# One gather for two sequences and an earlier transposition of K at the start of a block-sparse attention with a routed MLP

## The chip, the core and the metric

The kernel runs on one core of one Trainium2 chip, in float32. The metric is the device time of one execution in microseconds (us). A profiled execution gives the trace from which the details come.

## What is computed

Two stages follow each other. The first is BigBird attention over 4 sequences (batch), 8 heads, 768 positions and 64 features per head. Positions come in 24 blocks of 32. A query block sees its own block and both neighbours, the first and the last block, and three random blocks; the first and the last query block see everything.

```python
mask = np.abs(blk_i - blk_j) <= window
mask = mask | (blk_i == 0) | (blk_j == 0) | (blk_i == n_blocks - 1) | (blk_j == n_blocks - 1)
for qb in range(n_blocks):
    for kb in sampled_blocks[qb]:
        mask[qb*block:(qb+1)*block, kb*block:(kb+1)*block] = True
...
attn = np.exp(scores)
attn = attn / (np.sum(attn, axis=-1, keepdims=True) + 1e-09)
return np.matmul(attn, v)
```

The second stage takes the 3072 rows of 512 features, picks for each the expert (of 8) whose embedding has the largest cosine with it, and computes `gate * (relu(x @ w1[e]) @ w2[e])` with 1024 hidden features.

## The kernel before

The attention works in 24 steps, one for each chunk of 128 queries of one sequence. Sequences go in pairs: a step number maps to a chunk and to one of the two sequences of the pair. The order of the first steps is written out in `TURNS`: step 0 is chunk 0 of sequence 0, step 1 chunk 1 of sequence 0, step 2 chunk 0 of sequence 1, step 3 chunk 1 of sequence 1; after that the two sequences alternate. Steps are pipelined: in step s the scores of chunk s are made (`score_near`, lines 549 and 552, and `score_far`, line 574), those of chunk s-1 are multiplied with V (`weigh_near`, `weigh_far`, `weigh_ends`, all through line 629), normalized (`normalize`, lines 680 to 698), and those of chunk s-2 are turned (`turn_x`, line 706) and multiplied with the experts' embeddings (`chunk_logits`, line 717). For chunk 0, whose first block sees all keys, there are `score_ends` (lines 596 to 607) and `weigh_ends` too.

The program's order on each engine is the order in which the code is written; nothing reorders it. [...]

What feeds the steps:

- `load_k` and `turn_k`: K of a pair of heads comes into `kraw` (6 buffers) and is turned by 6 transposes on TensorE (line 500) into a PSUM tile of the ring "big", which has two buffers and also holds every score tile. DVE (even pairs) or ACT (odd pairs) copies it to `kt` (line 502); after the fourth pair of a sequence ACT copies the first and last block behind it (line 505). Pairs 0 to 3 are sequence 0, pairs 4 to 7 sequence 1. Before the change, pairs 4 to 7 are turned at the end of step 1.
- `gather_k`: K of the random blocks, copied within SBUF by DVE and POOL (lines 531, 535).
- `gather_v`: V of the random blocks straight from device memory into the ring `vg` (two buffers, one per chunk of a pair), one transfer for each random slot and each block (line 477), with the block number read into SP's registers first (line 377). The argument `i` limits it to one of the two sequences. A chunk has 4 blocks and 3 slots, so 12 transfers; chunk 0 has 6, as two of its blocks are not gathered.
- `load_v`: V in full, into `vt`, one tile for each chunk; `stack`, `stack_ends` and `near_v` copy from it what the neighbours and ends need.
- `load_q` and `turn_q`: Q into `qraw` (two buffers), turned on TensorE (line 513) and copied by DVE into `qt` (line 518).

All of these transfers except the first three of Q are issued from SP's queue by `fetch_all` (lines 475, 477, 479), which can put a load between each second gather. The queue ahead of the first steps is written out: gathers of chunk 0 for sequence 0; V tiles 2 to 5 of sequence 0; K of pairs 6 and 7; gathers of chunk 1 for sequence 0, with Q of sequence 1 between; V tiles 0 and 1 of sequence 1; gathers of chunk 0 for sequence 1; V tiles 2 to 5 of sequence 1; gathers of chunk 1 for sequence 1; a row of zeros to `x_dram` (line 1314). Behind them come step 2's loads: Q of the next chunks and K of pairs 8 and 9.

`build_experts` is a generator that is advanced between the steps: it normalizes the 8 embeddings and turns them (line 232) into `en`, in two halves that share one PSUM bank, each followed by a copy on DVE (line 234).

After the attention, expert tiles of 128 rows run (lines 1152 and 1165), with weights streamed from device memory.

Of the kernel before, what the change touches and what calls it, by code (L numbers as in the profile page):

```python
# [12 lines left out]
F32 = mybir.dt.float32  # L13
I32 = mybir.dt.int32
BF16 = mybir.dt.bfloat16
ACT = mybir.ActivationFunctionType
# [4 lines left out]
P = 128  # L21
# [4 lines left out]
NC = S // P  # L26
NPAIR = H // 2
N = B * S
NT = B * NC
DM, E, F = H * D, 8, 1024  # L30
ND, NF = DM // P, F // P
# [38 lines left out]
def bank(k, name):  # L70
    if k.attending:
        return ring(k, "yp", 0, 1, k.eps, [P, DM])
    return two_banks(k, name)[:, 0]
# [141 lines left out]
def build_experts(k):  # L215

    nc, pool = k.nc, k.setup
    emb, tau = k.emb_rows, k.tau_rows
    sq = pool.tile([E, DM], F32, name="emb_sq")
    nrm = pool.tile([E, 1], F32, name="emb_nrm")  # L220
    nc.scalar.activation(sq, emb, ACT.Square, accum_out=nrm)
    nc.gpsimd.tensor_tensor(out=nrm, in0=nrm, in1=k.half[0:E, 0:1], op=ALU.pow)
    yield
    nc.vector.tensor_scalar(out=nrm, in0=nrm, scalar1=1e-6, scalar2=tau[:, 0:1], op0=ALU.add, op1=ALU.mult)
    nc.vector.reciprocal(out=nrm, in_=nrm)
    nc.vector.tensor_scalar(out=emb, in0=emb, scalar1=nrm[:, 0:1], scalar2=None, op0=ALU.mult)
    yield
    k.en = k.const.tile([P, ND, E], F32, name="en")
    for some in (range(2), range(2, ND)):
        tp = bank(k, "tp")  # L230
        for c in some:
            nc.tensor.transpose(tp[:, c * E:(c + 1) * E], emb[:, c * P:(c + 1) * P], k.ident[0:E, 0:E])
        cols = slice(some.start * E, some.stop * E)
        nc.vector.tensor_copy(out=k.en.rearrange("p c e -> p (c e)")[:, cols], in_=tp[:, cols])
        yield


def load_pair(k, g, parts=(0, 1, 2)):
# [171 lines left out]
def load_q(k, s, i=None):  # L410

    a, c = pair_chunk(s)
    if ("q", s) not in k.raw:
        k.raw["q", s] = k.ld.tile([P, DUO, H, D], F32, name="qraw", tag="qraw", bufs=2)
    t, src = in_pair(k.raw["q", s], i), of_seq(k.q, a, i)
    return [(t[rows], src[lo:lo + rows.stop - rows.start]) for rows, lo in pieces(c)]
# [9 lines left out]
def load_v(k, a, m, i=None):  # L426

    v, src = in_pair(k.vt[m], i), of_seq(k.v, a, i)
    return [(v[rows, :, 0:D], src[lo:lo + rows.stop - rows.start]) for rows, lo in pieces(m)]
# [32 lines left out]
def gather_v(k, s, i=None):  # L462

    a, c = pair_chunk(s)
    t, src = k.vg_ring[s % 2], of_seq(k.v, a, i)
    for r in range(NRAND):
        for g, shift in zip(blocks_of(c), shifts(k, mybir.EngineType.SP, r, c)):
            yield in_pair(t[r * BLK:(r + 1) * BLK, g], i)[:, :, 0:D], src[bass.ds(shift, BLK)]


def fetch_all(k, gathers, loads):

    for i, (to, src) in enumerate(gathers):
        if i % 2 == 0 and loads:
            k.nc.sync.dma_start(out=loads[0][0], in_=loads[0][1])
            loads = loads[1:]
        k.nc.sync.dma_start(out=to, in_=src)  # L477
    for to, src in loads:
        k.nc.sync.dma_start(out=to, in_=src)
# [12 lines left out]
def turn_k(k, g):  # L492

    nc = k.nc
    b, j = divmod(g, NPAIR)
    kt = k.kt[b % 2]
    raw = k.raw.pop(("k", g))
    ps = k.big.tile([P, 2, 512], F32, name="kps", tag="big")
    for c in range(NC):
        nc.tensor.transpose(ps[:, c // 3, c % 3 * P:(c % 3 + 1) * P], raw[:, c].rearrange("p h d -> p (h d)"), k.ident)  # L500
    copy = nc.scalar.copy if g % 2 else nc.vector.tensor_copy
    copy(out=kt[:, j, 0:S].rearrange("p (w t) -> p w t", w=2), in_=ps[:, :, 0:3 * P])  # L502
    if j == NPAIR - 1:
        for i, block in enumerate((NB - 1, 0)):
            nc.scalar.copy(out=kt[:, :, S + i * BLK:S + (i + 1) * BLK], in_=kt[:, :, block * BLK:(block + 1) * BLK])  # L505
# [132 lines left out]
def weigh_near(k, n, turn):  # L638

    _, c, i = place(n)  # L640
    if turn == 0:
        k.av[n] = two_banks(k, "av"), set()
    e, st = k.pac[n], k.st_ring[n // DUO % 2]
    for hh in range(2 * turn, 2 * turn + 2):
        for h in (hh, hh + NPAIR):
            for half in (1,) if c == 0 else (0, 1):
                to = side(c, h, half)
                weigh(k, n, slice(D * to, D * (to + 1)), h, e[:, h // 2, half, D * (h % 2):D * (h % 2 + 1)],
                      st[:, half, i, h], turn == 1)
    if turn == 1:  # L650
        k.pac.pop(n)


def weigh_far(k, n, part):
# [14 lines left out]
def normalize(k, n):  # L669

    nc = k.nc
    b, c, i = place(n)
    s = n // DUO
    if i == 0:
        k.x[s] = k.xp.tile([P, DUO, ND, XE], F32, name="x", tag="x")
        k.nsq[s] = k.xp.tile([P, DUO], F32, name="nsq", tag="nsq")
        k.lg[s] = k.xp.tile([P, DUO, E], F32, name="lg", tag="lg")
    av = k.av.pop(n)[0].rearrange("p g (h w) -> p (g h) w", w=P)
    den = k.dens[:, n, :]
    nc.vector.tensor_scalar(out=den, in0=av[:, :, D], scalar1=1e-9, scalar2=None, op0=ALU.add)  # L680
    inv = k.xt_pool.tile([P, H], F32, name="inv", tag="inv")
    nc.vector.reciprocal(out=inv, in_=den)
    x = k.x[s][:, i, :, 0:P].rearrange("p j (h d) -> p j h d", h=2)
    half = NPAIR // 2
    if c:
        todo = [(slice(0, P), slice(0, P), slice(0, NPAIR))]
    else:
        todo = [(slice(0, P), slice(0, P), slice(0, half)), (slice(0, D), slice(D, P), slice(half, NPAIR)),
                (slice(D, P), slice(0, D), slice(half, NPAIR))]
    for to, at, pairs in todo:  # L690
        heads = slice(2 * pairs.start, 2 * pairs.stop)
        count = pairs.stop - pairs.start
        nc.vector.tensor_tensor(  # L693
            out=x[to, pairs], in0=av[at, heads, 0:D].rearrange("p (j h) d -> p j h d", h=2),
            in1=inv[at, heads].rearrange("p (j h) -> p j h", h=2).unsqueeze(3).broadcast_to(
                [at.stop - at.start, count, 2, D]), op=ALU.mult)
    sq = k.xt_pool.tile([P, ND, P], F32, name="sq", tag="sq", bufs=1)
    nc.scalar.activation(sq, k.x[s][:, i, :, 0:P], ACT.Square, accum_out=k.nsq[s][:, i:i + 1])


def turn_x(k, n):

    s, i = divmod(n, DUO)
    ps = ring(k, "xg_ps", 0, 1, k.eps, [P, ND, P])
    for j in range(ND):
        k.nc.tensor.transpose(ps[:, j], k.x[s][:, i, j, 0:P], k.ident)  # L706
    k.xt[n] = t = k.xt_pool.tile([P, ND, P], F32, name="xt", tag="xt")
    k.nc.vector.tensor_copy(out=t, in_=ps)  # L708
# [535 lines left out]
def attention_fast(n, ctx):  # L1244
# [3 lines left out]
    nc = n.nc  # L1248
# [36 lines left out]
    for vg in n.vg_ring:  # L1285
        nc.gpsimd.memset(vg[:, :, :, :, D:D + 1], 1.0)
    build_choice(n)
    fetch_all(n, gather_v(n, 0, 0), [])
    for m in range(2, NC):
        fetch_all(n, (), load_v(n, 0, m, 0))  # L1290
    turn_q(n, 0)
    for g in range(NPAIR):
        turn_k(n, g)
        if g + 6 < 2 * NPAIR:
            fetch_all(n, (), load_k(n, g + 6))
    fetch_all(n, gather_v(n, 1, 0), load_q(n, 0, 1) + load_q(n, 1, 1))
    for m in range(2):
        fetch_all(n, (), load_v(n, 0, m, 1))
    fetch_all(n, gather_v(n, 0, 1), [])
    for m in range(2, NC):  # L1300
        fetch_all(n, (), load_v(n, 0, m, 1))
    fetch_all(n, gather_v(n, 1, 1), [])
    build_bias(n)
    gather_k(n, 0)
    n.half = n.const.tile([P, NC], F32, name="half")
# [1 line left out]
    experts = build_experts(n)  # L1307
# [5 lines left out]
    nc.gpsimd.memset(zero, 0.0)  # L1313
    nc.sync.dma_start(n.x_dram[N:N + 1, :], zero)

    turning = {10: (8, 9), 11: (10, 11, 12), 12: (13, 14, 15)}
    keys_at = {2: (8, 9), 3: (10,), 4: (11,), 5: (12,), 6: (13,), 10: (14, 15)}
    values_at = {7: (0,), 8: (1,), 9: (2,), 11: (3,), 13: (4,), 15: (5,)}
    routed = {TURNS.index(DUO * b + 1) + 2: b for b in range(NS - 1)}
# [1 line left out]
    for s in range(NCH + 1):  # L1321
        now, after, last, past = (TURNS[i] if 0 <= i < NCH else None for i in (s, s + 1, s - 1, s - 2))
# [8 lines left out]
        def keys_gathered():  # L1331
            if after is not None:
                gather_k(n, after)

        ends = last is not None and place(last)[1] == 0
        late_keys = s == 1 or s in turning
        if now is not None:
            score_near(n, now)
            score_far(n, now)
# [26 lines left out]
            score_ends(n, last, 2)  # L1366
        if past is not None:
            turn_x(n, past)
        for g in turning.get(s, ()):
            turn_k(n, g)  # L1370
        if s in turning:
            keys_gathered()
        for part in range(2):
            if last is not None:
                weigh_far(n, last, part)
            if after is not None and part == 0 and not ends:
                turn_q(n, after)
        if ends:
            weigh_ends(n, last, (0, 2))
# [36 lines left out]
            build_consts(n)  # L1416
            next(experts)
        if s == 1:
            for g in range(NPAIR, 2 * NPAIR):
                turn_k(n, g)  # L1420
            keys_gathered()
            next(experts)
            next(experts)
            setup.close()
            n.dp = pool("dp_e", 1)
# [228 lines left out]
```

## Time and profile before

| | |
|---|---|
| median of 3 runs | 645.87 us (643.56 to 647.22) |
| profiled execution | 645.84 us |
| its span | 644.0 us |
| TensorE busy | 607.3 us, 94% of the span |
| DVE, ACT, POOL busy | 37%, 22%, 38% |
| mean granted TensorE clock | 0.976 |
| attention steps | up to about 290 us |
| DMA moved | 170.57 MB in 187,599 packets, 148,008 of them under 512 B |

The profile page gives busy times by engine, the chain of work that ended last, and groups of instructions by source line. A line of the timeline reads: start, length, engine, source line, operation, output<-inputs, shape, count, and in brackets the idle time before it with what ended it. "PE" is TensorE's matmuls (transposes among them), "PEld" its weight loads, "SPq" the issuing of DMAs by SP's queue: its length is the time that the queue was held, not that of the transfer.

### The profile page before, as it was taken

How to read it: one execution, taken by the hardware profiler on the slowest of the kernel's cores; microseconds unless marked ns; L12 is line 12 of the kernel's file. 1: busy time of each engine (PE TensorE's matmuls, PEld its weight loads, DVE VectorE, ACT ScalarE, POOL GpSimd, SP SyncE). 2: the span in 40 equal slices, each digit the busy share in tenths (PEclk: the TensorE clock that was granted, in tenths of full speed). 3: DMA queues.
4: the chain of work that ended last, by engine and by line, in shares of the span. 5: the costliest groups of instructions: out<-in, count | busy, mean ns of one | idle time of the engine just before them, and what ended most of it. 6: DMA issues, size and time to landing. Idle time of an engine off the chain costs nothing.

```text
span 644.0 us, 18357 instructions
## 1 busy us (share of the span) xinstructions
PE 607.3 (94%) x7496; PEld 471.4 (73%) x7496; DVE 235.6 (37%) x740; ACT 141.6 (22%) x286; POOL 244.5 (38%) x472
## 2 busy tenths in 40 slices
PE   6879889899999999999999999999999999999995
PEld 3668878798899888887777777663677746667773
DVE  3545544656666675236622111221121121211110
ACT  1534444554554444210000000000000000000000
POOL 1618246534766532031033444333334433333332
PEclk7899979999999799999999999999999999999998
DMA  9877999999999994079999999999899998999611
GB/s 170 170 150 152 177 170 170 183 185 175 182 191 184 178 162 145 36 278 401 396 406 394 406 399 365 341 320 375 308 395 410 396 375 308 413 390 408 247 48 34
DMA packets 187599, 170.57 MB, mean 265 GB/s; under 512 B 148008, under 2 KB 148136, under 8 KB 184690
## 3 DMA queue, kind: packets, MB, share of 16 engines
q1 hardware_dynamic: 180194, 155.35, 84.8%
q0 software_dynamic: 5216, 13.43, 5.7%
q8 instruction: 61, 1.00, 0.7%
q10 hardware_dynamic: 2096, 0.52, 0.5%
q14 instruction: 32, 0.26, 0.2%
HBM read 156.65 MB, written 12.90 MB: 263 GB/s over the span
## 4 chain that ended last, share of the span: by engine, by line
PE 75%; DMA 7%; SPq 6%; DVE 5%; issue 2%; POOL 2%; ACT 1%; POOLq 0%; DVEq 0%; ACTq 0%
PE hp L1152 25%; PE yp L1165 23%; PE av L629 6%; SPq L477 5%; PE dps L574 4%; PE yp L717 3%; DMA vg<-in_v_dram 3%; PE hp L1197 2%; PE yp L1217 2%; PE ac L549 2%; PE xg_ps L513 2%; PE ac L552 2%; DMA w<-in_moe_w_dram 2%; DMA qraw<-in_q_dram 1%; DMA kraw<-in_k_dram 1%
## 5 line engine op out<-in xcount | busy, mean ns | idle before, releaser
L1152 PEld LDWEIGHTS hp<-xgt,w 128*128 128x128 f32 x1472 | 167.8, 192 | 11.5 <-issue 10.2
L1152 PE MATMUL hp<-xgt,w 128*128 128x128 f32 x1472 | 169.2, 275 | 1.0 <-DMA w<-in_moe_w_dram 1.0
L1165 PE MATMUL yp<-w,h 128*128 128x512 f32 x368 | 161.9, 592 | 0.0
L1165 PEld LDWEIGHTS yp<-w,h 128*128 128x128 f32 x368 | 68.1, 190 | 76.5 <-issue 72.0
L1076 POOL DMA_INDIRECT xg<-x_dram,quarter x88 | 89.4, 1016 | 32.3 <-issue 27.4
L1178 POOL DMA_INDIRECT out_dram<-y,slot_l x20 | 20.5, 1026 | 155.8 <-DVE y L1177 155.8
L1155 ACT ACTIVATE h<-hp 128x512 f32<-128x512 f32 x23 | 13.7, 597 | 284.1 <-PE hp L1152 226.6
L1159 DVE TENSOR_SCALAR h<-hp 128x512 f32<-128x512 f32 x23 | 15.9, 692 | 145.1 <-PE hp L1152 145.1
L489 POOL COPY vg<-vt 32x1040 f32<-32x1040 f32 (+1 forms) x45 | 43.1, 958 | 57.2 <-PE av L629 45.0
L531 POOL COPY kg<-kt 128x128 f32 x176 | 43.2, 291 | 45.5 <-ACT kt L502 38.0
L549 PE MATMUL ac<-qt,kt 128*64 128x128 f32 x352 | 47.0, 290 | 3.3 <-DVE qt L518 3.3
L574 PEld LDWEIGHTS dps<-qt,kg 128*64 128x64 f32 x1408 | 48.2, 142 | 0.8 <-POOL vg L489 0.8
L574 PE MATMUL dps<-qt,kg 128*64 128x64 f32 x1408 | 46.9, 226 | 0.5 <-DVE kg L531 0.5
L552 PE MATMUL ac<-qt,kt 128*64 128x256 f32 (+1 forms) x192 | 46.4, 389 | 0.8 <-ACT kt L505 0.8
L518 DVE COPY qt<-xg_ps 64x512 f32<-64x512 f32 x48 | 33.0, 688 | 36.3 <-PE xg_ps L513 36.0
L1177 DVE TENSOR_SCALAR y<-yp,gate 128x512 f32<-128x512 f32 x20 | 15.0, 751 | 85.0 <-PE yp L1165 72.9
L549 PEld LDWEIGHTS ac<-qt,kt 128*64 128x64 f32 x352 | 41.5, 147 | 4.2 <-ACT st L441 1.8
L579 ACT ACTIVATE pd<-dps,bias 128x256 f32<-128x256 f32 x88 | 34.7, 475 | 15.8 <-PE dps L574 15.8
L629 PE MATMUL av<-vg,pd 128*32 128x65 f32 x1408 | 32.4, 225 | 3.5 <-DMA vg<-in_v_dram 2.8
L629 PE MATMUL av<-st,pac 128*64 128x65 f32 x704 | 31.0, 229 | 2.3 <-DVE x L693 1.3
L629 PEld LDWEIGHTS av<-vg,pd 128*32 128x32 f32 x1408 | 23.8, 110 | 12.1 <-issue 8.8
L708 DVE COPY xt<-xg_ps 128x512 f32<-128x512 f32 x24 | 16.6, 690 | 31.8 <-PE xg_ps L706 31.7
(229 smaller groups left out, 633.7 us busy)
## 6 DMA issues: line engine op xcount, KB each, us to landing
w<-in_moe_w_dram SPq DMA_DIRECT2D x52, 2048.0 KB
vg<-in_v_dram SPq DMA_DIRECT2D x114, 128.0 KB
kraw<-in_k_dram SPq DMA_DIRECT2D x32, 192.0 KB
x_dram<-x SPq DMA_DIRECT2D x10, 516.0 KB
qraw<-in_q_dram SPq DMA_DIRECT2D x9, 512.0 KB
w<-in_moe_w_dram SPq DMA_DIRECT2D x8, 512.0 KB
vt<-in_v_dram SPq DMA_DIRECT2D x10, 256.0 KB
vt<-in_v_dram SPq DMA_DIRECT2D x5, 512.0 KB
```

The lines of the kernel that those rows point to most:

```text
L477: k.nc.sync.dma_start(out=to, in_=src)
L489: k.nc.gpsimd.tensor_copy(out=k.vg_ring[s % 2][NRAND * BLK:P, g, which(i)], in_=k.vt[m][rows, which(i)])
L518: k.nc.vector.tensor_copy(out=t[rows, :, h], in_=ps[rows])
L531: copy(out=t[:, :, g, s * BLK:(s + 1) * BLK], in_=kt[:, :, bass.ds(shift, BLK)])
L549: nc.tensor.matmul(out[0:D, j, half], lhsT=kt[:, j, at:at + D], rhs=qt[:, j, :, D * half:D * (half + 1)], start=True, stop=True)
L552: nc.tensor.matmul(out[D:P, j, half:2].rearrange("p f h t -> p h f t"), lhsT=kt[:, j, S:S + D], rhs=qt[:, j, :, D * half:P].rearrange("p h ...
L574: nc.tensor.matmul(out[D * r:D * (r + 1), NG * j + g], lhsT=kg[:, j, g, D * r:D * (r + 1)], rhs=qt[:, j, :, cols], start=True, stop=True)
L579: nc.scalar.activation(e[:, :, g].rearrange("p j h t -> p j (h t)"), out.rearrange("p (j g) h t -> p j g (h t)", g=NG)[:, :, g], ACT.Exp, ...
L629: k.nc.tensor.matmul(av[lanes, h // NPAIR, h % NPAIR * P:h % NPAIR * P + D + 1], lhsT=lhsT, rhs=rhs, start=first[0], stop=last, skip_group ...
L1076: k.nc.gpsimd.indirect_dma_start(out=x[:, g], out_offset=None, in_=quarters, in_offset=bass.IndirectOffsetOnAxis(ap=k.quarter[:, g, t:t + ...
L1152: nc.tensor.matmul(hp[:, f, :], lhsT=w1[:, d, (f0 + f) * P:(f0 + f + 1) * P], rhs=xt[:, d, :], start=(d == 0), stop=(d == ND - 1))
L1165: nc.tensor.matmul(yp, lhsT=h[:, f, :], rhs=w2[:, f, :], start=(f == 0), stop=(f == NF - 1))
```

## The change

Three edits, and one that makes room. (a) `gather_v` is called without `i` for the first two chunks, so that one transfer brings a block for both sequences (32 rows x 16 heads x 64 features instead of 32 x 8 x 64); V of sequence 1 follows all gathers. (b) K of sequence 1 is turned in the middle of steps 0 (pairs 4, 5) and 1 (pairs 6, 7), where before all four pairs were turned at the end of step 1; in step 0 `turn_q` moves ahead of it, and in step 1 the gather of K for step 2 follows it. (c) The embeddings are turned into one PSUM bank at once and copied once. The squares that `normalize` makes only for their sum are written over the used probabilities (`pac`) instead of a tile of their own.

```diff
-    for some in (range(2), range(2, ND)):
-        tp = bank(k, "tp")
-        for c in some:
-            nc.tensor.transpose(tp[:, c * E:(c + 1) * E], emb[:, c * P:(c + 1) * P], k.ident[0:E, 0:E])
-        cols = slice(some.start * E, some.stop * E)
-        nc.vector.tensor_copy(out=k.en.rearrange("p c e -> p (c e)")[:, cols], in_=tp[:, cols])
-        yield
+    tp = bank(k, "tp")
+    for c in range(ND):
+        nc.tensor.transpose(tp[:, c * E:(c + 1) * E], emb[:, c * P:(c + 1) * P], k.ident[0:E, 0:E])
+    nc.vector.tensor_copy(out=k.en.rearrange("p c e -> p (c e)"), in_=tp[:, 0:ND * E])
+    yield
...
-    if turn == 1:
-        k.pac.pop(n)
...
-    sq = k.xt_pool.tile([P, ND, P], F32, name="sq", tag="sq", bufs=1)
-    nc.scalar.activation(sq, k.x[s][:, i, :, 0:P], ACT.Square, accum_out=k.nsq[s][:, i:i + 1])
+    used = k.pac.pop(n)[:, 0:NPAIR:2].rearrange("p j f w -> p j (f w)")
+    nc.scalar.activation(used.rearrange("p j (e w) -> p j e w", w=P),
+                         k.x[s][:, i, :, 0:P].rearrange("p (j e) w -> p j e w", e=2), ACT.Square,
+                         accum_out=k.nsq[s][:, i:i + 1])
...
-    fetch_all(n, gather_v(n, 0, 0), [])
+    fetch_all(n, gather_v(n, 0), [])
...
-    fetch_all(n, gather_v(n, 1, 0), load_q(n, 0, 1) + load_q(n, 1, 1))
-    for m in range(2):
+    fetch_all(n, gather_v(n, 1), load_q(n, 0, 1) + load_q(n, 1, 1))
+    for m in range(NC):
         fetch_all(n, (), load_v(n, 0, m, 1))
-    fetch_all(n, gather_v(n, 0, 1), [])
-    for m in range(2, NC):
-        fetch_all(n, (), load_v(n, 0, m, 1))
-    fetch_all(n, gather_v(n, 1, 1), [])
...
-    turning = {10: (8, 9), 11: (10, 11, 12), 12: (13, 14, 15)}
+    turning = {0: (4, 5), 1: (6, 7), 10: (8, 9), 11: (10, 11, 12), 12: (13, 14, 15)}
...
-        late_keys = s == 1 or s in turning
+        late_keys = s in turning and s > 0
...
+        if s == 0:
+            turn_q(n, after)
         for g in turning.get(s, ()):
             turn_k(n, g)
-        if s in turning:
+        if late_keys:
             keys_gathered()
         for part in range(2):
             if last is not None:
                 weigh_far(n, last, part)
-            if after is not None and part == 0 and not ends:
+            if after is not None and s and part == 0 and not ends:
                 turn_q(n, after)
...
         if s == 1:
-            for g in range(NPAIR, 2 * NPAIR):
-                turn_k(n, g)
-            keys_gathered()
-            next(experts)
             next(experts)
```

## Prediction

> **What bounds the kernel now.** I read the chain of waits first. Most of it is TensorE work, with a DMA share, and 6% of the span in which the chain runs through SP's own queue, nearly all in line 477, the V gathers.
>
> ```profile
> PE 75%; DMA 7%; SPq 6%; DVE 5%; issue 2%; POOL 2%; ACT 1%; POOLq 0%; DVEq 0%; ACTq 0%
> ```
>
> Next came windows over the places where TensorE (PE) falls idle. Columns: stretch, its length, busy us (instructions) of PE, weight loads, DVE, ACT, POOL, then PE's granted clock, DMA share, GB/s.
>
> ```profile
> 40.00:47.00 7.00, 3.91 (x39) 3.36 (x37) 4.84 (x14) 2.70 (x6) 1.63 (x7) 1.00 0.67 144
> 61.00:67.00 6.00, 4.01 (x109) 3.57 (x108) 0.00 (x0) 1.72 (x3) 2.17 (x3) 1.00 0.84 183
> 83.00:87.00 4.00, 1.82 (x36) 1.14 (x35) 0.78 (x2) 2.77 (x5) 3.71 (x11) 1.00 1.25 185
> 87.00:94.00 7.00, 7.00 (x81) 6.61 (x81) 3.81 (x15) 0.99 (x4) 0.62 (x3) 0.52 1.34 169
> ```
>
> PE has holes at 40-47, 61-67 and 83-87, and right after the third its clock is about half for 7 us while it is fully busy. The timeline of PE names the holes (start, length, line, idle before it and its releaser):
>
> ```profile
> 37.70 0.63 PE L513 MATMUL xg_ps<-ident,qraw 128*128 128x128 f32 x4 [1.54 <-DMA qraw<-in_q_dram]
> ...
> 40.04 1.53 PE L500 MATMUL kps<-ident,kraw 128*128 128x128 f32 x12
> 42.94 1.53 PE L500 MATMUL kps<-ident,kraw 128*128 128x128 f32 x12 [1.37 <-DVE kt L502]
> 44.40 0.29 PE L232 MATMUL yp<-ident,emb 8*128 8x8 f32 x2
> 46.40 0.29 PE L232 MATMUL yp<-ident,emb 8*128 8x8 f32 x2 [1.72 <-DVE en L234]
> ```
>
> ```profile
> 83.76 0.27 PE L629 MATMUL av<-vg,pd 128*32 128x65 f32 x2 [0.54 <-DMA vg<-in_v_dram]
> 84.66 0.27 PE L629 MATMUL av<-vg,pd 128*32 128x65 f32 x2 [0.62 <-DMA vg<-in_v_dram]
> 85.40 0.27 PE L629 MATMUL av<-vg,pd 128*32 128x65 f32 x2 [0.47 <-DMA vg<-in_v_dram]
> 86.22 0.61 PE L629 MATMUL av<-vg,pd 128*32 128x65 f32 x26 [0.54 <-POOL kg L531]
> ```
>
> At 40-47 four K transposes and the two embedding halves stand in a row at the end of step 1, and step 2 starts its scores only at 46.62. The fourth row at 86 is named for POOL, but its weight load also waits on the last gather (landed 86.08 by the trace's semaphore updates), so I count all four, 2.2 us, as gathers that came late. Why they were late shows in SP's timeline:
>
> ```profile
> 48.60 3.07 SPq L479 DMA_DIRECT2D vt<-in_v_dram  x4
> 51.87 9.04 SPq L477 DMA_DIRECT2D vg<-in_v_dram  x12
> 61.01 0.29 SPq L1314 DMA_DIRECT2D x_dram<-zero  x1
> 61.39 0.41 SPq L479 DMA_DIRECT2D qraw<-in_q_dram  x1
> ```
>
> Four 256 KB loads leave in 3.07 us, but twelve 64 KB gathers take 9.04, 0.75 us each, while the 16 DMA engines are only 0.63 busy at 53-61. SP's issuing is the limit there. Behind it stands the q load of step 2, which leaves at 61.39 and lands at 66.93; PE waits 1.91 us for it at 67.06.
>
> **What the skill says.** "DMA: Bandwidth & Descriptors", section Rules for kernel authors: many small transfers should be coalesced, since "under 64 KB you're paying mostly overhead". This trace agrees: 0.75 us of queue for 64 KB against 0.77 for 256 KB. "Perfetto Trace Analysis", DMA Instruction — HWDGE: the recorded time of an issue covers lock, descriptor generation and semaphore push, not the data movement. Agrees: the q load issues in 0.41 us and lands 5.5 us after. "TensorE: Matmul & The Clock Gate", Part 1, says PE's clock halves after an idle window of about 3.4 us and is judged in free-running windows of 3413 ns. The trace agrees in form: the clock records hold half speed from 87.25 to 94.08, twice 3.41 us, right after the window 83.84-87.25 in which PE was 52% busy. But windows of 51% and 55% (42.88-46.29, 36.05-39.46) were not followed by it, so the threshold is not plain.
>
> **The change, part by part.** The sum is made against the profiled execution: 645.84 us, span 644.0, so 1.8 around it; the median of the three runs is 645.87, the same within 0.1.
>
> *Gathers for both sequences.* 36 gathers of 64 KB become 18 of 128 KB, and two of the eight register loads on SP (median 0.39) go. The shortest issue is 0.316 us in both sizes (the gathers of 19-61, and the 128 KB ones of 82-130); with 0.18 us of register work each pair of issues is 0.50 us apart when nothing blocks. Upper bound: 18 x 0.50 + 0.8 = 9.8 us of SP queue saved. Lower bound: none, if a transfer costs by its bytes. By bytes, 128 KB take 0.58 us (256 B packets take 18-19 ns on each of 16 engines), so the set stays near its issue rate and I take 7.5. The q load of step 2 then leaves near 54 and lands near 59. PE wants it at 65.15 minus what it gains before, so 3 us of saving suffice. The six gathers of chunk 0 now carry 384 KB more ahead of K of pairs 6 and 7; they leave at their old times (19.1 to 22.7, set by register loads), the data end about 0.4 us later. Packet count and bytes stay.
>
> *V of sequence 1* moves behind all gathers: its last load leaves near 47 instead of 51.7, its first near 42.5 as now. Wanted at 58: nothing.
>
> *K of pairs 4, 5 in step 0.* PE 2 x 0.77 after the q transposes at 22.56-23.22. Cover: PE idles 1.57 there for DVE's q copies (end 24.64). But step 1's first scores now need the PSUM buffer that DVE empties with the copy of pair 4, 0.96: first scores at 25.75 for 24.79, +0.95.
>
> *K of pairs 6, 7 in step 1*, ahead of weigh_far, in PE's queue in front of everything else of the step. The score_ends before it finish at 31.23, now 32.2. The semaphore updates put the landing of pair 6 at 33.03 and of pair 7 at 35.65. So PE waits 0.9, turns 0.75, waits 1.9, turns 0.75: weigh_far starts at 36.6, not 31.16, +5.4 (the +0.95 is inside it, hidden by the wait). Queued behind: weigh_far, weigh_ends, score_ends, the next q. The q transposes no longer wait 1.54 (q lands near 38.5, wanted at 41.6), but the last weigh_ends waits some 0.25 for ACT's Exp, which that wait had covered: +4.1 at the end of step 1. DVE and ACT take 0.96 and 0.80 for each copy beside PE, and the K gathers on POOL (15.1 us idle before 45.37) and DVE come earlier: free; with that cover gone a copy would cost its 0.96 or 0.80.
>
> *What goes at the end of step 1.* From 40.04 to 46.62, 6.58 us, shrink to the four embedding transposes in one go, 0.6 (no wait for a DVE copy between). So step 2's scores start at 46.62 + 4.1 - 6.0 = 44.7, -1.9. Late next is DVE: normalize ends at 45.9, then 2.3 us of K copies to 48.4 before the x copy, which PE reaches at 47.9; the q transposes wait 0.6 more. **-1.3** at step 3.
>
> *The wait for q at 67.06* goes: **-1.9**. *The vg waits at 83-86* go, as SP starts those gathers when step 3 frees the buffer (near 59) and not at 68.2 behind its backlog: -2.2, less 0.2 for the x copy they covered: **-2.0**. A vg wait of 0.77 at 124.5 mostly goes: **-0.6**.
>
> *The clock.* Without the hole at 83-87 I expect no half clock behind it. In 87-94 groups take 1.75 to 1.9 times their usual time (L717 1.81 for 0.99, L629 1.07 for 0.62), so 6.8 us do what 3.8 would: **-3.0**. But the new hole at 32-36.5 has PE busy 26 to 45% of any 3.4 us window, less than the 52% that was followed by half clock, and dense work follows: **+3.0**, taken as somewhat likelier than not.
>
> *The square into pac*: same engine, 512 elements, 0.63 us as now, no new wait (ACT writes both tiles, in order), beside PE's next scores: 0; without that cover its 0.63 per step.
>
> Sum: -1.3 - 1.9 - 2.0 - 0.6 - 3.0 + 3.0 = -5.8, **640.0 us**. The experts' stage is PE-bound and shifts along.
>
> **Rivals.**
> 1. *No half clock from the new hole* (window phase is free, so it can fall either way): 637.0. For: windows at 51-55% stayed fast.
> 2. *The old half clock stays, or DVE and POOL take up what the vg waits gave* (POOL's K copies ran to 86.8, 7.5 us before PE needed them; that slack shrinks to about 2): 642.5 to 643.5.
> 3. *The gather costs by bytes*: SP saves nothing, the waits at 67 and 83 stay, only -1.3 is left, no more than measurement noise: 644.5. For: many 128 KB issues take 0.5 to 1.0 (median 0.57 in 82-130). Against: those run with full DMA engines.
> 4. *Slower: K arrives late in step 1.* Each us that pair 7 lands after 35.65 is a us on PE, as nothing passes the transposes in its queue. By bytes, 384 KB at the 170 GB/s of that stage are 2.2 us. With the half clock (+3.0), and the later waits unchanged, the sum is -1.3 + 2.2 + 3.0 = +3.9: 649.7. It decides from a landing at about 37.2.
> That the change does not do what it says is out: the compiled instruction lists show the moved transposes, 18 gathers of 32x16x64, and one embedding copy.
>
> **Chances.** Forecast 0.36, rival 1 0.26, rival 2 0.13, rival 3 0.16, rival 4 0.09. A run of this kernel can tell about 0.5%, 3.2 us, from no change, so faster means below 642.6: forecast, rival 1 and the better half of 2, 0.70; same 0.22; slower 0.08. The range, 636.0 to 645.0, takes in rivals 1 to 3 and leaves out rival 4 and stray ends.
>
> **What would show it.** Right: 18 gathers in the first two chunks about 0.5 us apart, q of step 2 issued near 54; kps waits on DMA kraw near 33 and 35; step 2's scores near 45 (later with a half clock); no DMA wait at PE near 67 or 83; no half clock in the nineties. Wrong: step 2's scores after 47 without a half clock, gathers 1 us apart, or the vg waits back in place.

## The result and the profile after

The changed kernel takes 638.42 us (median of 4 runs, 636.15 to 639.11) beside 645.20 for the kernel before on the same chip: ratio 0.9887, 95% interval 0.9848 to 0.9927. The profiled execution took 639.11 us with a span of 637.4, so it is compared with 645.84 and 644.0: 6.6 us of span. In the changed kernel a source line stands 1 or 2 numbers lower (transposes of K L498, of Q L511, products with V L627).

The chain of waits has nearly the same shares as before; it doesn't show the gain:

```profile
PE 75%; DMA 8%; SPq 6%; DVE 5%; ACT 2%; issue 2%; POOL 0%; DVEq 0%; POOLq 0%
```

The windows over the places shown before (61-67, 83-87, 87-94), and one that is new (37-41). "Half clock" below means that the granted clock in the records is 0.50 of full speed:

```profile
37.00:41.00 4.00, 3.83 (x70) 3.36 (x72) 0.93 (x4) 1.30 (x3) 1.53 (x7) 0.57 0.93 154
61.00:67.00 6.00, 5.87 (x144) 5.26 (x132) 1.10 (x3) 2.24 (x3) 5.68 (x12) 1.00 0.88 190
83.00:87.00 4.00, 4.00 (x84) 3.72 (x83) 2.76 (x8) 1.87 (x4) 2.39 (x9) 1.00 0.98 147
87.00:94.00 7.00, 6.81 (x187) 6.13 (x185) 4.44 (x20) 3.15 (x9) 2.94 (x8) 1.00 1.31 168
```

The holes at 61-67 and 83-87 are filled (PE 5.87 for 4.01, 4.00 for 1.82). From 87 to 94 the clock is 1.00 for 0.52, and 187 matmuls fit where 81 did. In exchange 37-41 runs at 0.57. PE's timeline shows the hole ahead of it:

```profile
33.74 0.85 PE L498 MATMUL kps<-ident,kraw 128*128 128x128 f32 x6 [0.94 <-ACT pb L605]
37.17 1.40 PE L498 MATMUL kps<-ident,kraw 128*128 128x128 f32 x6 [2.59 <-DMA kraw<-in_k_dram]
...
47.12 0.32 PE L547 MATMUL ac<-qt,kt 128*64 128x128 f32 x1
```

Pair 7 of K landed at 37.04, not 35.65. TensorE (PE) stood idle 2.59 us for it. Behind these transposes in its queue stood `weigh_far`, which in the kernel before ran at 31.16. Step 2's scores begin at 47.12, where the kernel before has 46.62. SP's queue after the change:

```profile
38.40 7.14 SPq L475 DMA_DIRECT2D vg<-in_v_dram  x8
45.60 8.93 SPq L477 DMA_DIRECT2D vt<-in_v_dram  x7
55.14 0.38 SPq L477 DMA_DIRECT2D qraw<-in_q_dram  x1
```

Before, eight gathers of half the size in the same place took

```profile
36.46 5.92 SPq L477 DMA_DIRECT2D vg<-in_v_dram  x8
```

Q for step 2 leaves at 55.14 instead of 61.39 and lands at 60.70; nothing waits for it. Eight joined gathers held the queue for 0.89 us each, register loads included, for 0.74 before, and more than the 0.50 of the prediction. The seven V loads behind them held it for 8.93 us; in the kernel before the same loads took 4.59 (1.52 for three at 42.43, 3.07 for four at 48.60).

The table lays the executions side by side. It takes the Q transposes of a step, names them by their start in the kernel before, and gives how much later (+) or earlier (-) they start in the changed kernel. The last column is a second profiled execution of the changed kernel, of which more below.

| start before, us | changed kernel, us | the same once more, us |
|---|---|---|
| 37.7 (step 1) | +6.3 | +3.4 |
| 50.5 | +0.5 | -0.2 |
| 67.1 | -1.5 | -2.2 |
| 75.7 | -1.4 | -2.2 |
| 86.8 | -4.2 | -4.9 |
| 98.2 | -7.3 | -8.0 |
| 106.5 | -5.9 | -7.2 |
| 116.5 | -4.2 | -6.0 |
| 126.0 | -5.0 | -5.9 |
| 202.3 | -3.2 | -5.0 |
| 223.4 | -6.9 | -8.7 |

What was gained by 98 is partly given back between 98 and 116, in two places. The first is gathers of V that land late:

```profile
99.28 0.30 PE L627 MATMUL av<-vg,pd 128*32 128x65 f32 x2 [0.65 <-DMA vg<-in_v_dram]
100.00 0.61 PE L627 MATMUL av<-vg,pd 128*32 128x65 f32 x26 [0.42 <-DMA vg<-in_v_dram]
```

The second is a store. PE, DVE and SP there:

```profile
109.67 0.69 PE L627 MATMUL av<-st,pac 128*64 128x65 f32 x16 [2.66 <-DVE x L804]
```

```profile
108.83 0.69 DVE L689 TENSOR_TENSOR x<-av,inv 128x512 f32<-128x512 f32 x1 [4.98 <-DMA x_dram<-x]
```

```profile
99.19 4.58 SPq L475 DMA_DIRECT2D vg<-in_v_dram  x4
103.88 0.90 SPq L813 DMA_DIRECT2D x_dram<-x  x2
```

`normalize` writes a tile of the ring x, which has three buffers, and waits until an older tile's store to `x_dram` has landed (108.75). The last write of that store's data ended at 95.8, but SP issued it at 103.88, behind K loads and gathers. Before, the same wait was 3.25 us and cost PE 0.93:

```profile
113.88 0.69 PE L629 MATMUL av<-st,pac 128*64 128x65 f32 x16 [0.93 <-DVE x L806]
```

Now the steps reach it 5.9 us earlier and SP issues the store only 3.3 us earlier (103.88 for 107.22), and it costs PE 2.66.

The last jump, -3.2 to -6.9, is no step of the change. It is a half clock in the execution of before:

```profile
213.50:220.50 7.00, 7.00 (x80) 6.97 (x82) 5.02 (x21) 2.02 (x5) 6.21 (x17) 0.51 1.22 205
```

Against this one execution, even the run below that gains nothing (turns only) falls from +4.4 to +1.2 there. The prediction's sum is thus best judged up to 202 us, and the total by medians.

### The profile page after: what moved, and what is told of

Same layout as the page of the kernel before. It is cut to its first block, busy times and chain, and to the rows that moved or that the text cites. A ratio compares the mean times of both kernels' runs of the same rounds, so it can differ in the third digit from the quotient of the medians.

```text
span 637.4 us, 18298 instructions
## 1 busy us (share of the span) xinstructions
PE 602.4 (95%) x7496; PEld 466.4 (73%) x7496; DVE 235.0 (37%) x739; ACT 142.6 (22%) x286; POOL 243.5 (38%) x472
## 4 chain that ended last, share of the span: by engine, by line
PE 75%; DMA 8%; SPq 6%; DVE 5%; ACT 2%; issue 2%; POOL 0%; DVEq 0%; POOLq 0%
PE hp L1150 25%; PE yp L1163 24%; PE av L627 7%; SPq L475 4%; PE dps L572 3%; DMA kraw<-in_k_dram 3%; DMA vg<-in_v_dram 3%; PE yp L715 2%; PE hp L1195 2%; PE yp L1215 2%; PE ac L547 2%; DMA w<-in_moe_w_dram 2%; PE ac L550 2%; PE xg_ps L511 1%; PE bps L594 1%
## 5 line engine op out<-in xcount | busy, mean ns | idle before, releaser
L547 PE MATMUL ac<-qt,kt 128*64 128x128 f32 x352 | 42.9, 274 | 2.6 <-DVE qt L516 1.4
L550 PE MATMUL ac<-qt,kt 128*64 128x256 f32 (+1 forms) x192 | 42.4, 364 | 1.1 <-ACT kt L503 1.1
L547 PEld LDWEIGHTS ac<-qt,kt 128*64 128x64 f32 x352 | 37.8, 137 | 3.5 <-DVE kt L500 1.4
L627 PE MATMUL av<-vg,pd 128*32 128x65 f32 x1408 | 33.2, 225 | 3.2 <-DMA vg<-in_v_dram 1.9
L627 PE MATMUL av<-st,pac 128*64 128x65 f32 x704 | 30.2, 225 | 4.0 <-DVE x L804 2.7
L627 PEld LDWEIGHTS av<-vg,pd 128*32 128x32 f32 x1408 | 24.0, 110 | 12.7 <-issue 8.5
L627 PEld LDWEIGHTS av<-st,pac 128*64 128x64 f32 x704 | 24.9, 137 | 4.8 <-issue 4.3
```

Of the source, the lines that this page charges most:

```text
L547: nc.tensor.matmul(out[0:D, j, half], lhsT=kt[:, j, at:at + D], rhs=qt[:, j, :, D * half:D * (half + 1)], start=True, stop=True)
L550: nc.tensor.matmul(out[D:P, j, half:2].rearrange("p f h t -> p h f t"), lhsT=kt[:, j, S:S + D], rhs=qt[:, j, :, D * half:P].rearrange("p h ...
L627: k.nc.tensor.matmul(av[lanes, h // NPAIR, h % NPAIR * P:h % NPAIR * P + D + 1], lhsT=lhsT, rhs=rhs, start=first[0], stop=last, skip_group ...
```

## The experiments

Each was timed beside the kernel before (medians 645.35, 644.83 and 645.54 in the three groups); the ratios, with 95% intervals, come from all runs and are not quotients of the medians. The first two split the change.

**Gathers only.** The kernel before with joined gathers and V of sequence 1 behind them; K and embeddings untouched.

```diff
-    fetch_all(n, gather_v(n, 0, 0), [])
+    fetch_all(n, gather_v(n, 0), [])
...
-    fetch_all(n, gather_v(n, 1, 0), load_q(n, 0, 1) + load_q(n, 1, 1))
-    for m in range(2):
+    fetch_all(n, gather_v(n, 1), load_q(n, 0, 1) + load_q(n, 1, 1))
+    for m in range(NC):
```

> The kernel before with only the gathers joined (and V of sequence 1 behind them); K of sequence 1 and the embeddings as before. Theory A (the gathers bring nearly all, the earlier K turn pays its gain back in a new wait and a half clock): PE's q wait at 67 and vg waits at 83 are gone, no half clock at 87 and none at 37, step 2's scores near 46.9 as before; a DVE wait on the x_dram store near 108 of 3.5 to 5 us; 5 to 6.5 us under before, so 639 to 640. Rival B (the row of K turns at the end of step 1 was the cost, the gathers were hidden behind PE): at most 1.5 us under before, 644 or more.

640.38 us, ratio 0.992 (0.989 to 0.9949). The waits at 67 and 83 and the half clock at 87 are gone. At the start it is worse: the Q that step 1 turns lands at 39.79, where the kernel before has 37.56. PE waits 4.00 us for it, for 1.54 before, and runs at half clock from 38.83 to 45.66:

```profile
39.93 1.09 PE L513 MATMUL xg_ps<-ident,qraw 128*128 128x128 f32 x4 [4.00 <-DMA qraw<-in_q_dram]
```

So the Q transposes that stood at 50.5 come 4.1 us late; those that stood at 98 come 3.7 early. This run joins the gathers and moves V of sequence 1 behind them; the two were not tried apart.

**Turns only.** The changed kernel with the four gather calls of before and V of sequence 1 between them. It keeps the embeddings in one step and the squares in `pac`, so it tests parts (b) and (c) of the change without part (a).

```diff
-    fetch_all(n, gather_v(n, 0), [])
+    fetch_all(n, gather_v(n, 0, 0), [])
...
+    fetch_all(n, gather_v(n, 0, 1), [])
...
+    fetch_all(n, gather_v(n, 1, 1), [])
```

> The changed kernel with the gathers as in the kernel before: only K of sequence 1 turned in steps 0 and 1, embeddings in one step, squares into pac. Theory A: PE waits for K of pair 7 in step 1 until about 35.7, some 2 us in all; step 2's scores at 45 to 47.5 depending on whether half clock follows; the q wait near 67 and the vg waits near 83 stay, half clock behind them as well: 643 to 647, within 2 us of before. Rival B: 5 us or more under before, 640 or less.

646.16 us, ratio 1.000 (0.9979 to 1.002). The Q transposes of 50.5 come 2.4 us earlier, and then PE stands still for what SP has not yet issued:

```profile
68.09 1.09 PE L511 MATMUL xg_ps<-ident,qraw 128*128 128x128 f32 x4 [5.35 <-DMA qraw<-in_q_dram]
```

The clock is half from 65.27 to 75.51. An earlier step without an earlier queue was worth nothing here.

**Later turn of K in step 1.** Pairs 6 and 7 behind `score_ends(1)`, `(3)`, ahead of `turn_q`, so that the wait for K has work in front of it.

```diff
-        for g in turning.get(s, ()):
-            turn_k(n, g)
-        if late_keys:
-            keys_gathered()
+        if s != 1:
+            for g in turning.get(s, ()):
+                turn_k(n, g)
+            if late_keys:
+                keys_gathered()
...
             score_ends(n, last, 1)
             score_ends(n, last, 3)
+            if s == 1:
+                for g in turning[s]:
+                    turn_k(n, g)
+                keys_gathered()
```

> The changed kernel with K of pairs 6 and 7 turned later in step 1, behind the last score_ends and ahead of the q transposes, where K has long landed. Theory A: no wait for kraw and no half clock at 37; step 2's scores near 44 instead of 47.1. But the store of x to x_dram leaves SP behind its backlog at an unchanged time near 104, so the wait of DVE for its landing grows by what PE gained, from 5 to about 8 us, and the end moves by 0 to 1.5 us only: 637 to 638.4. Rival C (from step 2 on PE's own work is the limit and the gain runs through to the end): 3 us or more under the changed kernel, 635.5 or less.

636.62 us, ratio 0.9861 (0.9831 to 0.989). The interval overlaps that of the change, so it is not shown to be better. The profiled execution is the slowest of the six (639.27). In it the wait for K is gone, step 2's scores begin at 42.75, and the gain is lost earlier than expected, at the gathers of chunk 1, with half clock from 51.01 to 54.42 behind them:

```profile
48.36 0.27 PE L627 MATMUL av<-vg,pd 128*32 128x65 f32 x2 [2.53 <-DMA vt<-in_v_dram]
49.26 0.27 PE L627 MATMUL av<-vg,pd 128*32 128x65 f32 x2 [0.63 <-DMA vg<-in_v_dram]
50.24 0.30 PE L627 MATMUL av<-vg,pd 128*32 128x65 f32 x2 [0.70 <-DMA vg<-in_v_dram]
51.05 1.07 PE L627 MATMUL av<-vg,pd 128*32 128x65 f32 x26 [0.52 <-DMA vg<-in_v_dram]
```

The trace names `vt` for the first, but gathers landed at 48.22, 49.13, 50.19 and 51.01, and each of the four products starts 0.04 to 0.14 us after one of them.

**The hole filled.** Ten products of zeros ahead of the turn of pair 7 (they go to a spare bank and serve nothing).

```diff
         for g in turning.get(s, ()):
+            if g == 7:
+                spare = bank(n, "spare")
+                for _ in range(10):
+                    nc.tensor.matmul(spare, lhsT=n.zeros[:, 0:P], rhs=n.zeros, start=True, stop=True)
             turn_k(n, g)
```

> The changed kernel with ten matmuls of zeros into a spare bank, ahead of the turn of pair 7 in step 1, where TensorE stood idle for K (adds work, changes no result). Theory H (the idle hole at 32 to 37 causes the half clock of 37.3 to 40.7): no half clock there, step 2's first scores 1.5 to 1.8 us earlier than 47.1, near 45.5, unless the filling itself ends later than K's landing at 37.0; the later gains of the change pass part of it on, time 636.5 to 638. Rival T (the half clock comes with the time or the load of that stretch, not the hole): half clock stays, step 2's scores at 47 or later, time 638.4 to 640.

```profile
34.21 2.32 PE L1369 MATMUL yp<-zeros 128*128 128x512 bf16 x10
36.37 0.82 PE L498 MATMUL kps<-ident,kraw 128*128 128x128 f32 x6
...
48.55 0.30 PE L627 MATMUL av<-vg,pd 128*32 128x65 f32 x2 [0.46 <-DMA vg<-in_v_dram]
49.74 0.48 PE L627 MATMUL av<-vg,pd 128*32 128x65 f32 x18 [0.89 <-DMA vg<-in_v_dram]
```

The half clock at 37 is gone, which theory H asked for, and step 2's scores begin at 44.77, 2.35 us earlier. But 1.35 of that is waited away for V at 48-50, and the time is 639.53 (0.9926, 0.9892 to 0.996): no gain. K landed at 35.53 in this run, before the zeros were done (36.37, where the transposes start), so it can't be told whether the filling or the earlier K kept the clock up.

**The changed kernel once more.**

> The changed kernel once more, beside the three others: 638.4 within 1 us. Its profile should show the same waits (K at 34-37, DVE's for the store of x at 104-109) and the same half clock at 37-41, and no fixed place for the half clocks after 100 us; one near 140-160 or 208-220 would say that their absence in the first profile was chance.

637.42 us, ratio 0.9887 (0.9853 to 0.992). In this profile pair 7 landed at 35.65, where the prediction put it:

```profile
35.79 0.84 PE L498 MATMUL kps<-ident,kraw 128*128 128x128 f32 x6 [1.39 <-DMA kraw<-in_k_dram]
...
44.22 0.32 PE L547 MATMUL ac<-qt,kt 128*64 128x128 f32 x1
...
48.46 0.30 PE L627 MATMUL av<-vg,pd 128*32 128x65 f32 x2 [0.87 <-DMA vg<-in_v_dram]
49.70 0.64 PE L627 MATMUL av<-vg,pd 128*32 128x65 f32 x26 [0.94 <-DMA vg<-in_v_dram]
```

```profile
37.00:41.00 4.00, 4.00 (x127) 3.61 (x116) 0.92 (x4) 1.62 (x4) 2.93 (x12) 1.00 1.41 184
```

The clock stays at 1.00, so the expectation that the half clock at 37 would come again was wrong. The clock records come in windows of 3.41 us; with K 1.4 us earlier the two windows over the hole (31.65 to 38.47) have PE 58% and 79% busy, where the window ahead of the half clock in the first profile (33.90 to 37.31) has 24%. No filling was needed: a smaller hole goes with the full clock, which speaks for theory H without proving it. The store wait came again (DVE 4.4, PE 2.10 us). Between 100 and 630 us neither profile of the change has a half clock, so that it is chance isn't shown for this kernel; variants had some, such as at 113 and 208 (fourth buffer), at 143 and 208 (hole filled) and at 157 (later turn).

**Gathers for chunk 1 in halves again**, sequence 1's half behind Q in step 2, with the later turn of K and without it.

```diff
-    fetch_all(n, gather_v(n, 1), load_q(n, 0, 1) + load_q(n, 1, 1))
+    fetch_all(n, gather_v(n, 1, 0), load_q(n, 0, 1) + load_q(n, 1, 1))
...
-        if s == 3:
+        if s == 2:
+            gathers = gather_v(n, 1, 1)
+        elif s == 3:
             gathers = gather_v(n, ahead)
```

> The later turn of K in step 1, and the gathers of chunk 1 again for one sequence at a time: sequence 0's where they were, sequence 1's behind the load of Q in step 2. Chunk 0's stay joined. Theory B (the joined gathers of chunk 1 carry sequence 1's half, 768 KB, ahead of its need through DMA engines that are full from 31 to 51 us, and it is their bytes for which TensorE waits at 45-51 with the later turn, 4.4 us and 1.7 of half clock): those waits go, step 2's weigh_near starts 3 to 5 us earlier, and if the later gathers don't come late, 632 to 635. Rival S (SP's issuing is the limit: twelve more issues): the waits come back at 67 or 83 as waits for Q or V, and the time is 637 or above.

> The changed kernel with the gathers of chunk 1 for one sequence at a time as in the run above, and the turn of K where the change has it. TensorE's wait for pair 7 of K (landed 37.0) is ahead of these gathers in the queue and stays, with its half clock of 37 to 41. Theory B: step 2's scores at 47 as before, nothing gained there or lost later, 637.5 to 639. Rival S: as in the run above, above 640.

643.16 us (0.9968, 0.9949 to 0.9988) and 642.44 (0.9954, 0.9935 to 0.9972). Each theory named one half of what the first of them shows. As theory B says, PE has no wait for V at 45-51 and is 4.4 us ahead of the kernel before at the Q transposes of 50.5, 6.4 at 67. As rival S says, the next gathers, behind twelve more issues, come late:

```profile
82.65 0.40 PE L627 MATMUL av<-vg,pd 128*32 128x65 f32 x2 [5.76 <-DMA vg<-in_v_dram]
```

```profile
80.50:94.00 13.50, 10.08 (x115) 8.76 (x117) 4.06 (x17) 0.99 (x4) 0.78 (x4) 0.50 1.39 167
```

5.76 us of wait and 13.65 us of half clock take the 6.4 away within two steps. In the second the waits of 83 are back at 81-85 (0.83, 0.48, 0.55, 0.49 us). Both runs keep V of sequence 1 where the change has it and lose over half of the gain, which speaks for the joining and against that order as the cause. It isn't proof, as they also move sequence 1's gathers behind Q.

**Gathers and one embedding**, without the moved turns.

```diff
             keys_gathered()
             next(experts)
-            next(experts)
```

The embeddings' new form and the gather calls are as in the change.

> The kernel before with the joined gathers and the embeddings in one step; K of sequence 1 is turned at the end of step 1 as before. With gathers alone: 640.4. The embeddings' DVE wait, 1.7 us at the end of step 1, goes. If that row is on the path, 638.7, and the moved turn of K is worth next to nothing (the changed kernel has 638.4). If V's landing at 50 takes its place, as it did where the hole was filled, 640.4 stays.

638.87 us, ratio 0.9904 (0.9879 to 0.9929). In the same group the changed kernel has 0.9887 (0.9853 to 0.992): this is the time of the change within its uncertainty, without the turns. Whether the embeddings' 1.5 us against gathers only are real can't be told: the intervals overlap.

**Two ways at the store of x.** On ACT's queue, and with a fourth buffer (the tile of zeros that the warm-up multiplies was halved to make room, and the number of its products doubled).

```diff
-        nc.sync.dma_start(out=dram[lo:lo + rows.stop - rows.start], ...
+        nc.scalar.dma_start(out=dram[lo:lo + rows.stop - rows.start], ...
```

> The changed kernel with the stores of x to x_dram issued from ACT's queue instead of SP's. Theory A (the store is late because it stands behind gathers in SP's queue): it leaves near 96, when its data are ready, instead of 103.9; DVE's wait for it near 104 to 109 is gone, PE's wait of 2.66 at 107 shrinks under 0.7, and the time falls by 2 to 2.7 us: about 636. Rival D (the 16 DMA engines are full there, so the store lands as late from whichever queue, or what is gained is given back as vg waits): within 0.7 us of the changed kernel, 638.

655.66 us, ratio 1.0157 (1.0118 to 1.0196): slower, with a wait that no theory had. The longest of SP's waits from 84 to 104, and the two gathers between which it stood:

```profile
SPq L475 <- DMA x_dram<-x: 11.1, 1, 11.1
```

```profile
87.53 12.08 SPq L475 DMA_DIRECT2D vg<-in_v_dram  x2
```

The second of these gathers signals the same completion semaphore as the store that ACT had been given; it was issued at 99.30, 20 ns after that store landed (99.28). Half clock from 103.02 to 113.26 follows. How the 17 us lost against the changed kernel divide between the two isn't shown, and the run says nothing on the buffer wait.

```diff
-    k.x[s] = k.xp.tile([P, DUO, ND, XE], F32, name="x", tag="x")
+    k.x[s] = k.xp.tile([P, DUO, ND, XE], F32, name="x", tag="x", bufs=4)
```

> The changed kernel with four buffers instead of three for the tile x, so that normalize need not wait for a store of x to x_dram that stands behind gathers in SP's queue. Theory A (the store's late issue ends DVE's wait at 104-109, and through it PE's idle 2.66 us at 107): both waits go, and with nothing else late next the time falls by 2 to 2.5 us, to about 636. Rival G (the 2.7 us are given back as gathers of V that come late, since SP's queue is what is behind there): PE's wait at 107 is gone, but waits on vg of about the same sum appear within the next 20 us, and the time stays within 0.7 us of the changed kernel, 637.7 to 639.

638.33 us, ratio 0.9901 (0.9869 to 0.9934). DVE's wait and PE's 2.66 are gone; 0.5 us of V waits at 120 and a wait of 1.88 at 109, for which the trace names no releaser, take their place, with a half clock at 113-116. As rival G has it, nothing is gained, though not all of it is shown to have gone to gathers.

The later turn and the fourth buffer together:

> The later turn of K in step 1 (behind score_ends, as in the run before with that edit, 636.6) together with four buffers for x. If the two waits are independent, their gains add: 636.6 less 2 to 2.5, about 634.4. If the queue of SP is the common limit, it gives one gain only: 636 to 637.

637.85 us, ratio 0.9911 (0.9878 to 0.9945): the two don't add. In the profile PE waits 3.81 us for V of chunk 1 at 45-51, and half clock follows from 48.42 to 58.66.

And with Q first:

```diff
-    fetch_all(n, gather_v(n, 1), load_q(n, 0, 1) + load_q(n, 1, 1))
+    fetch_all(n, (), load_q(n, 0, 1))
+    fetch_all(n, gather_v(n, 1), load_q(n, 1, 1))
```

> As the run before, and the first load of Q for step 2 stands ahead of the gathers of chunk 1 instead of among them. The gathers of chunk 1, for which PE waited 4.4 us at 45-51 with the later turn, then leave about 0.4 us later. If the queue's issue sets their landing, PE waits longer by some 0.4 us, and the time is that of the run before or 0.5 above. If Q's landing was what turn_q waited for, it is up to 1 us lower.

639.58 us, ratio 0.9911 (0.988 to 0.9942). V's waits at 46-50 were 2.80 us, for 3.81 in the run before it, so Q first didn't lengthen them; the median is higher and the interval nearly the same. No variant is shown to beat the change.

## Why the prediction was right, step by step

Forecast 640.0; measured 638.42 and 637.42. The side and the main cause of the gain hold. Several terms of the sum were mis-sized and one loss was missing, and these errors partly cancel, so that the number comes so close is in part luck. The range, 636 to 645, also holds rivals 1 to 3; the waits below say more than the range does.

*The queue.* 7.5 us saved was 6.25 (61.39 to 55.14). The step "the set stays near its issue rate" failed. A joined gather of chunk 1 did not cost 0.50 to 0.58 us, but 0.84 by the spacing of its landings (44.51 to 50.40 for eight), and its issues stood 0.95 us apart (38.40 to 45.02), nearly the 1 us that the prediction named as a sign of being wrong. The windows from 35 to 52 us, before and after, show why:

```profile
35.00:52.00 17.00, 12.18 (x278) 10.54 (x277) 9.82 (x26) 6.39 (x12) 6.39 (x23) 1.00 0.71 153
35.00:52.00 17.00, 14.74 (x344) 12.86 (x348) 6.78 (x23) 5.01 (x11) 2.94 (x12) 0.90 1.11 164
```

The DMA engines' share rose from 0.71 to 1.11 while the rate only rose from 153 to 164 GB/s, and each of the eight gathers landed 5 to 6 us after its issue, for 2 to 4 before. An estimate from these figures (share x 16 engines x 256 B / rate) gives 19 ns for a 256 B packet before and 28 ns after. The prediction took its 0.58 us from the packets of the less busy trace. So there the joined gathers do cost by their bytes, as rival 3 has it; what saved the forecast is that 3 us of queue were enough. For chunk 0, with register loads between them, six took 3.99 us for 3.92 with twice the bytes. The Trainium skill, "DMA: Bandwidth & Descriptors", Rules for kernel authors, advises to coalesce many small transfers into one large one. The runs agree for SP's queue: gathers only gave 0.8%, and splitting chunk 1 again raised the ratio from 0.9887 to 0.9954.

*Step 1.* The wait for K was predicted with a landing at 35.65 and a delay of 5.4 us. It landed at 37.04 and 35.65 in the two profiles; rival 4's point, 37.2, was nearly reached once. Step 2's scores were put at 44.7 without a half clock and came at 44.22 in the profile that has none. The -1.3 behind it failed: "late next is DVE" named the wrong thing. Late next is V of chunk 1. Its last gather lands at 50.40 and 49.66 in the two profiles, for 44.52 before, when only one sequence's half went ahead. So PE reaches the Q transposes of 50.5 at +0.5 us with the half clock and at -0.2 without it, 0.7 apart, though step 2's scores are 2.9 apart. On top of the gathers and the one embedding step the turns of K show no gain: 638.87 us without them, 637.42 with them in the same group, and the intervals overlap.

*The waits.* Each measured figure is a difference between two rows of the table above, first profile. The wait for Q at 67 was predicted as -1.9 and gave 2.0 (+0.5 to -1.5). The waits for V at 83-86 were predicted as -2.0 and gave 2.8 (-1.4 to -4.2). The half clock behind them was predicted as -3.0 and gave 3.1 (-4.2 to -7.3). All three came as described. The -0.6 at 124.5 is -0.8 in the first profile (-4.2 to -5.0) and nothing in the second.

*The new half clock*, +3.0: one window of 3.41 us in the first profile, by estimate 1.7 us (half of the window), and none in the second. The prediction took two windows from the case at 87. The second profile is the case of rival 1. Most of the cost is hidden by V's landing, as the 0.7 us above show: the two profiled executions took 639.11 and 637.69, 1.4 apart, where the forecast and rival 1 stand 3.0 apart.

*Not predicted:* what is given back from 98 to 116, 3.1 us of 7.3 in the first profile and 2.0 of 8.0 in the second. Of this, 1.4 and 0.8 lie where gathers of V land late near 99, and 1.7 and 1.2 at the store of x, which stands behind gathers in SP's queue (PE's wait of 2.66 and 2.10 for 0.93 before). The prediction asked what is late next at some of the removed waits, but did not follow the steps, which now run ahead of the queue, to the next transfers that they need. And the half clock at 213-220 in the execution of before, about 3.7 us, was in the profile and was not seen as something that the execution after may lack. Ahead of it, at 202 us, the two profiles of the change are 3.2 and 5.0 us early, less than the sum's 5.8; the medians give 6.8 and 8.1. Single executions can't close that gap.

The gain is shown to come from part (a) of the change, the joined gathers with V of sequence 1 behind them, and parts (b) and (c) alone gave nothing. What each smaller part adds, below some 2 us, stays open, as does the exact share of the half clocks.

## What to carry over

Where one queue feeds everything and runs late, look at what limits it. Here it was the number of issues at first, and once those were joined, the bytes. Moving compute forward only changed which transfer was waited for: cost a moved step by when its last input lands, for the next two steps too. A joined transfer takes the second half's bytes ahead of need; look where they stand in front of something urgent, and weigh that against the issues saved. A duration read in a less busy stretch need not hold once the change fills that stretch. Single profiles differ by several us through half clocks: compare step by step up to each of them, and take the total from medians.

## What the runs showed of the hardware

- The place of a half clock is not fixed, and how busy PE was in the window before, by the profile's modelled times, tells it only in part. The Trainium skill, "TensorE: Matmul & The Clock Gate", Part 1, speaks of an idle window and of free-running windows of 3413 ns. The traces agree on the windows: half clocks lasted 3.41, 6.83, 10.24 or 13.65 us. On what counts as idle they say less. From 30 to 290 us, every window of at most 37% was followed by half clock (24% in the first profile after, 32% at 45-48 with the later turn and fourth buffer, 0% at 77-80 in the later turn with split gathers). Above that, both happen: 42% at 105.6-109.0 in the first profile after was not followed, nor 49% at 38.2-41.7 (gathers and one embedding), while 52% at 83.8-87.2 in the kernel before, 60% at 109.5-112.9 (fourth buffer) and 76% at 153.4-156.8 (later turn) were. How long it lasts varied from one window (first profile after, with full work behind it) to four (13.65 us, after the empty window); in the kernel before it lasted two (87.25 to 94.08), though PE was busy throughout the first.
- Landing times of one K load in the same kernel differed by 1.4 us between two executions (37.04 and 35.65), and the half clock at 37 came only in the one with the later landing.
- A store given to ACT's queue held up SP's queue for 11.1 us, through a completion semaphore that both used. Moving this transfer to another queue did not uncouple the two.
